# Fused attention and feed-forward kernel: one transfer for the values of the first two groups, with the order around it laid anew

## The chip, the cores and the metric

One Trainium2 chip; the program runs on one core. That core has a matrix engine (TensorE, PE in the profile), a vector engine (VectorE, DVE), an activation engine (ScalarE, ACT), a general one (GpSimd, POOL) and a sequencer that mostly starts transfers (SyncE, SP). Each of them works through its own list of instructions strictly in order. The metric is device time in microseconds (us) of one execution; lower is better.

## The reference

Attention with normalised queries and keys for 8 batches of 12 heads, 448 positions, head size 64, followed by a two-layer feed-forward block with a leaky ReLU:

```python
q_n = q / (norm(q) + 1e-06);  k_n = k / (norm(k) + 1e-06)
scores = q_n @ k_n.T / tau                      # tau = 0.1
attn = exp(scores - max);  attn = attn / (sum(attn) + 1e-09)
x = (attn @ v)                                  # heads laid side by side: 3584 x 768
h = x @ w_in                                    # 768 -> 2048
out = maximum(0.01 * h, h) @ w_out              # 2048 -> 768
```

Inputs and output are float32 in memory. Since query and key rows have length one, the kernel leaves out the subtraction of the maximum.

## The kernel before

The work is cut into many small steps, each a Python function that issues a few instructions, and one long string, `ORDER`, lists all steps of the whole run. A loop at the end of the kernel takes the names one after the other (`k.3.2` calls `scores(3, 2)`). Each engine gets its instructions in the order of the string, and the framework adds the waits that the data need. So an instruction can be held by its own data, or by one ahead of it on its engine. There is no other planning at run time.

The names that matter here. A *slot* s is a pair of heads of one batch (slots 0 to 11, the first two batches, six slots each; from slot 12 on a slot carries the queries or the keys of two pairs). A *group* j is four heads, that is slots 2j and 2j+1. A *chunk* c is 384 columns (even) or 512 columns (odd) of tokens.

- `lq.s` loads queries and keys of a slot (SP; slots 0 to 5 are loaded ahead of the string by L652 to L660, in the order of the slots). There are four buffers, so from slot 10 on the load waits until `no` of an earlier slot has read its buffer.
- `lv.j` loads the values of group j (POOL starts it; L255). The three buffers are used in turn. `lr.b.lo.hi` loads the last 64 rows of the values of batch b for heads lo to hi-1 of each group, one transfer a head (L263). `lg.g` loads values for later groups (L281).
- `wi.i` loads a quarter of w_in (POOL; L181): i = 0, 1 are the even and odd row tiles for blocks 0 to 7, i = 2, 3 for blocks 8 to 15. `wo.half.lo.hi` loads w_out (L187); `wo.0` the columns 0 to 383, `wo.1.0.8` and `wo.1.8` the two parts of the rest.
- `sq.s.part` squares (POOL; part 0 the queries, 1 the keys, L305; L299 later), `su.s.part` adds the squares up (DVE, L318, L315), `ro.s` takes logarithm and exponential of the sums (ACT, L335 and L336), `no.s` normalises (DVE, L341 to L359). `qf`, `uf` and `sa` are the same for the first slots on ACT and DVE.
- `tp.s` transposes on PE (L375), `tc.s` copies the result out of PSUM (DVE, L391; `ta` on ACT). Later slots use `tt.s` (DVE, L401) and `td.u`, six transfers on SP (L410).
- `k.s.i` computes scores (PE, L428), `x.s.i` their exponentials (ACT, L439). `to.j` adds up the exponentials of a group and `pr.j.e` multiplies them with the values (PE, L451); `ln.j`, `in.j` make the inverse of the sums (ACT, L463, L467), `sc.j.e` scales into the tile xT (DVE, L479).
- For later groups `q.u.i` (PE, L493), `y.u.i` (ACT, L501), `g.g` and `g.g.e` (PE, L525, L539), `gl.g`, `gi.g` (ACT, L547, L551), `gx.g.e` (DVE, L565, L571) do the same.
- `f.c.m` is block m of the first layer (PE, L589): six products, one for each row tile of xT; `f.c.m.0.2` does only row tiles 0 and 2. Row tile 2j+e is what `sc.j.e` wrote. `r.c.m` is the ReLU into hT (ACT, L603). `s.c.ts.lo.hi` is the second layer (PE, L625), sixteen products over all blocks of the chunk; `o` copies it out (DVE, L641) and, when the row block is complete, stores it (SP, L649).
- `w.n` issues n products on constant data (L696), which fill PE's list while data are on the way. `hs.s` lets SP's list, `hp.s` POOL's, wait until `no.s` is done (L702, L705). `tg` ends a rule on which PSUM banks are dealt out.

PSUM has eight banks. A step that needs one or two takes those that were given back longest ago in the order of the string, and its first product waits until the step that gave them back has run. `k`, `q` and `g` need two at once, `f`, `s`, `tp`, `to`, `pr` one.

Of the kernel before, what the change touches and what calls it, by code (L numbers as in the profile page):

```python
# [13 lines left out]


ORDER = """
lq.6 qf.0.0.3 qf.0.3.4 uf.0.0.3 tg sq.2.1 qf.1.0.3 uf.0.3.4 sq.2.0 w.20 lr.0.0.2 uf.1.0.3 sq.3.1 lv.0 ro.0
sa.1.0 sq.3.0 no.0 sa.1.1 tp.0.4.7 tp.0.0.4 w.2 w.2 su.1.1 su.1.0 ta.0.0.4 tc.0.4.7 su.2.1 sq.4.1 lr.0.2.4
k.0.1 k.0.2 ro.1 k.0.0 no.1 w.2 w.2 w.2 su.2.0 lv.1 x.0.2 sq.4.0 sq.5.1 wi.0 lv.2 tp.1 tc.1 k.1.0 x.0.0 x.0.1
ro.2 x.1.0 su.3.1 no.2 k.1.2 k.1.3 w.2 lq.7 sq.5.0 su.3.0 lq.9 lq.8 x.1.2 k.1.1 x.1.3 ro.3 w.2 tp.2 w.3 tc.2  # L20
su.4.1 no.3 x.1.1 k.2.2 k.2.1 to.0 tp.3 k.2.0 su.4.0 x.2.2 wi.1 x.2.1 w.2 tc.3 ln.0 ro.4 x.2.0 sq.7.1 k.3.0
su.5.1 no.4 k.3.2 k.3.1 in.0 x.3.2 x.3.1 x.3.0 su.5.0 pr.0.1 tp.4 sq.6.1 sq.6.0 k.3.3 pr.0.0 tc.4 sc.0.1 k.4.0
ro.5 x.3.3 no.5 x.4.0 to.1 ln.1 k.4.2 tp.5 k.4.1 su.6.0 su.6.1 tc.5 x.4.2 ro.6 sq.9.1 pr.1.0 k.5.1 x.4.1 in.1
no.6 sc.0.0 sc.1.0 pr.1.1 x.5.1 k.5.2 sq.7.0 tp.6 x.5.2 tc.6 k.5.0 f.0.1.0.2 wi.2 sc.1.1 k.5.3 k.6.2 x.5.0
x.5.3 su.7.1 su.7.0 su.9.1 sq.9.0 su.9.0 sq.8.0 wi.3 k.6.0 x.6.2 to.2 sq.8.1 x.6.0 ro.7 pr.2.0 pr.2.1 ln.2
k.6.1 x.6.1 su.8.1 no.7 lq.10 f.0.3.0.1.2.3 f.0.1.1 f.0.1.3 f.0.0.0.2 in.2 sc.2.0 sc.2.1 f.0.0.1 f.0.0.3
f.0.2.0.1.2.3 f.0.4 tp.7 wo.0 f.0.2.4.5 su.8.0 ro.8 f.0.3.4.5 r.0.2 f.0.6 f.0.1.4.5 f.0.0.4.5 tc.7 no.8 ro.9
r.0.6 f.0.7 lq.11 tp.8 wo.1.0.8 lr.1.0.4 sq.10.0 sq.10.1 r.0.3 r.0.1 r.0.0 r.0.4 k.7.3 k.7.2 no.9 x.7.3 x.7.2
tc.8 lv.3 sq.11.1 sq.11.0 tp.9 tc.9 su.10.1 su.10.0 ro.10 r.0.7 f.0.15 lq.13 lq.12 f.0.9 f.0.5 f.0.11 sq.12
r.0.15 r.0.9 no.10 r.0.5 k.9.0 k.7.1 k.8.2 r.0.11 f.0.12 x.9.0 r.0.12 x.8.2 tp.10 f.0.10 tc.10 su.11.0 su.11.1  # L30
x.7.1 f.0.14 hs.9 hp.10 sq.13 k.10.0 k.7.0 k.8.1 r.0.14 x.7.0 f.0.8 f.0.13 x.8.1 ro.11 r.0.10 no.11 wo.1.8
to.3 su.13 su.12 r.0.13 x.10.0 r.0.8 ln.3 ro.13 ro.12 hs.11 s.0.0.0.384 tp.11 o.0.0.0.384 k.9.1 k.10.2 k.9.3
lq.15 s.0.2.0.384 no.13 tc.11 no.12 lq.14 x.9.3 x.10.2 x.9.1 sq.15 tt.12 k.11.2 k.8.0 tt.13 x.8.0 o.0.2.0.384
k.9.2 s.0.1.0.384 lv.4 k.11.1 td.0 x.9.2 in.3 x.11.2 k.11.3 k.10.1 hp.11 sq.14 hp.12 x.11.1 x.11.3 lv.5 pr.3.0
to.4 pr.3.1 k.11.0 sc.3.0 o.0.1.0.384 su.15 lq.16 s.0.2.384.768 su.14 s.0.1.384.768 o.0.2.384.768 hp.13 sq.16
lq.17 x.10.1 x.11.0 ln.4 ro.15 in.4 q.0.1 q.0.6 no.15 sc.3.1 q.0.2 ro.14 o.0.1.384.768 pr.4.1 to.5 tt.15 y.0.6
lq.18 y.0.2 su.16 pr.5.0 ln.5 in.5 y.0.1 pr.5.1 pr.4.0 sc.4.1 sc.5.0 no.14 ro.16 sc.4.0 q.0.4 q.0.5 tt.14
sc.5.1 td.1 lq.19 s.0.0.384.768 no.16 f.1.2 hp.15 sq.18 su.18 f.1.14 f.1.1 hp.16 sq.17 lg.0 su.17 sq.19 lq.21
r.1.2 ro.18 y.0.4 y.0.5 ro.17 f.1.8 o.0.0.384.768 f.1.10 r.1.1 r.1.8 r.1.14 r.1.10 f.1.11 q.1.6 q.0.3 q.1.5
f.1.12 no.17 r.1.11 y.0.3 y.1.6 f.1.6 lq.20 tt.17 tt.16 r.1.12 y.1.5 q.0.0 q.1.4 q.1.3 y.0.0 su.19 no.18 hp.17  # L40
sq.20 ro.19 y.1.3 y.1.4 f.1.5 f.1.13 f.1.3 no.19 q.1.1 r.1.6 r.1.13 r.1.5 g.0 q.1.2 y.1.1 q.1.0 r.1.3 gl.0
tt.18 tt.19 su.20 f.1.4 f.1.0 f.1.7 sq.21 td.2 f.1.9 lq.22 td.3 lq.23 y.1.0 f.1.15 su.21 ro.21 ro.20 r.1.0
r.1.15 r.1.7 r.1.9 r.1.4 y.1.2 gi.0 g.0.0 q.2.0 s.1.0.0.384 y.2.0 gx.0.0 q.2.2 q.2.1 q.2.3 no.21 o.1.0.0.384
no.20 tt.20 s.1.1.0.384 s.1.0.384.768 tt.21 lq.24 td.4 lq.25 o.1.1.0.384 sq.23 hp.19 sq.22 y.2.2 lg.1 su.22
y.2.1 q.2.4 y.2.3 hp.20 y.2.4 q.2.5 q.2.6 y.2.5 y.2.6 s.1.1.384.768 o.1.1.384.768 ro.22 s.1.2.0.384
o.1.2.0.384 no.22 tt.22 lq.26 hp.22 sq.24 su.23 q.3.0 y.3.0 g.1 gl.1 q.3.1 q.3.2 y.3.1 o.1.0.384.768 y.3.2
gi.1 ro.23 s.1.2.384.768 o.1.2.384.768 no.23 q.3.3 y.3.3 g.1.0 gx.1.0 tt.23 td.5 lq.27 hp.23 sq.25 su.24 q.3.4
q.3.5 y.3.4 y.3.5 ro.24 s.1.3.0.384 o.1.3.0.384 q.3.6 y.3.6 g.1.1 gx.1.1 q.4.0 q.4.1 y.4.0 y.4.1 lg.2
# [52 lines left out]
def kernel(  # L101
# [145 lines left out]

    vb, vrb = {}, []

    def load_v(j):  # L250
# [4 lines left out]
        gp.dma_start(out=vb[j], in_=main(v, b, 4 * jj, 4))  # L255
# [510 lines left out]
```

## Time and profile before

| | us |
|---|---|
| median of three runs (lowest to highest) | 416.45 (416.26 to 416.78) |
| the profiled execution, its own time | 415.89 |
| its span, first to last instruction | 414.1 |
| PE busy | 404.9 |
| DVE busy | 259.4 |
| ACT busy | 245.8 |
| POOL busy | 113.2 |
| PE's last product ends (from the span's start) | 411.0 |

The profile was taken by the hardware's profiler. Times in it count from the start of the span. "Busy" is time in which an engine executes; PE's is a little generous, since its products overlap. The granted TensorE clock is full over the whole span. Bandwidth over the first 78 us is 200 to 310 GB/s nearly throughout; the transfers that POOL starts run on one queue (called q0) and those of SP on another (q1), both served by the same sixteen engines.

The chain of work that ended last, followed back from the end, is 84% PE, most of it second-layer and first-layer products:

```profile
PE 84%; DMA 9%; SPq 2%; POOL 1%; ACT 1%; DVE 1%; issue 0%; POOLq 0%
```

How long the transfers took from their start to their landing, read for single ones by line: the first values (`lv.0`, started at 12.7 us) 6.0 us, `lv.1` (16.6) 5.5, `lv.2` (20.0) 8.9; the four quarters of w_in (19.2, 21.8, 28.6, 31.4) 8.7, 11.2, 9.6 and 11.3; `wo.0` (33.0) 21.9, `wo.1.0.8` (33.8) 24.5, `wo.1.8` (55.3) 12.4; keys of slot 5 (10.4) 4.8.

### The profile page before, as it was taken

How to read it: one execution, taken by the hardware profiler on the slowest of the kernel's cores; microseconds unless marked ns; L12 is line 12 of the kernel's file. 1: busy time of each engine (PE TensorE's matmuls, PEld its weight loads, DVE VectorE, ACT ScalarE, POOL GpSimd, SP SyncE). 2: the span in 40 equal slices, each digit the busy share in tenths (PEclk: the TensorE clock that was granted, in tenths of full speed). 3: DMA queues.
4: the chain of work that ended last, by engine and by line, in shares of the span. 5: the costliest groups of instructions: out<-in, count | busy, mean ns of one | idle time of the engine just before them, and what ended most of it. 6: DMA issues, size and time to landing. Idle time of an engine off the chain costs nothing.

```text
span 414.1 us, 11068 instructions
## 1 busy us (share of the span) xinstructions
PE 404.9 (98%) x4679; PEld 212.4 (51%) x4679; DVE 259.4 (63%) x424; ACT 245.8 (59%) x431; POOL 113.2 (27%) x120
## 2 busy tenths in 40 slices
...
GB/s 188 254 217 213 242 214 219 174 220 124 71 172 174 210 111 54 184 225 106 96 135 161 170 156 167 84 206 83 2 90 79 86 40 0 2 72 6 2 115 76
DMA packets 41974, 53.81 MB, mean 130 GB/s; under 512 B 12484, under 2 KB 32324, under 8 KB 41924
## 3 DMA queue, kind: packets, MB, share of 16 engines
q1 hardware_dynamic: 25732, 41.01, 35.1%
...
q10 hardware_dynamic: 688, 0.30, 0.3%
q14 instruction: 14, 0.11, 0.1%
...
## 4 chain that ended last, share of the span: by engine, by line
PE 84%; DMA 9%; SPq 2%; POOL 1%; ACT 1%; DVE 1%; issue 0%; POOLq 0%
PE ps L625 35%; PE ps L589 32%; PE ps L539 8%; PE ps L493 7%; DMA w_out_sb<-in_moe_w_out_dram 5%; DMA qk_h<-in_k_dram 3%; PE ps L451 2%; DMA xT<-in_q_dram 1%; POOL sq L305 1%; DVE xT L571 1%; PE ps L525 1%; PE ps L428 1%; ACT hT L603 0%; SPq L210 0%; SPq L218 0%; SPq L240 0%
## 5 line engine op out<-in xcount | busy, mean ns | idle before, releaser
L625 PE MATMUL ps<-w_out_sb,hT 128*128 128x384 bf16 (+1 forms) x912 | 151.7, 324 | 0.5 <-DMA w_out_sb<-in_moe_w_out_dram 0.5
L589 PE MATMUL ps<-xT,w_in_sb 128*128 128x384 bf16 (+1 forms) x768 | 151.0, 353 | 0.2 <-DMA w_in_sb<-in_moe_w_in_dram 0.2
L501 ACT ACTIVATE pe<-ps 128x896 bf16<-128x896 f32 x126 | 109.7, 917 | 53.3 <-PE ps L493 53.1
L625 PEld LDWEIGHTS <-hT 128*128 128x128 bf16 x912 | 86.5, 98 | 64.5 <-issue 10.8
L589 PEld LDWEIGHTS <-w_in_sb 128*128 128x128 bf16 x768 | 73.3, 98 | 73.3 <-issue 7.5
L603 ACT ACTIVATE hT<-ps 128x384 bf16<-128x384 f32 (+1 forms) x128 | 63.9, 549 | 64.0 <-PE ps L589 46.0
L299 POOL TENSOR_TENSOR sq<-qk_h 128x896 f32<-128x896 f32 x36 | 64.2, 1786 | 86.8 <-DMA qk_h<-in_k_dram 51.2
L641 DVE COPY osb<-ps 128x384 f32<-128x384 f32 (+1 forms) x57 | 30.7, 543 | 76.9 <-PE ps L625 73.2
L349 DVE TENSOR_TENSOR qn<-qk_h,r 128x896 bf16<-128x896 f32 x36 | 43.8, 1216 | 1.3
L315 DVE TENSOR_REDUCE ss<-sq 128x14 f32<-128x910 f32 x36 | 38.2, 1071 | 4.6 <-POOL sq L299 4.4
L439 ACT ACTIVATE pe<-ps 128x896 bf16<-128x896 f32 x42 | 36.0, 917 | 3.3 <-PE ps L428 3.2
L493 PE MATMUL ps<-qkT 64*32 64x448 bf16 x1008 | 36.6, 353 | 0.6 <-DVE xT L571 0.6
L509 DVE TENSOR_TENSOR shared<-shared,pe 128x896 f32<-128x896 f32 x30 | 35.2, 1207 | 0.3
L565 DVE TENSOR_TENSOR xT<-ps,rb 128x448 bf16<-128x448 f32 x32 | 18.3, 615 | 20.4 <-ACT rb L551 12.4
L401 DVE STREAM_TRANSPOSE tt<-qn 128x448 f32<-128x448 f32 x36 | 28.5, 812 | 0.5
L539 PE MATMUL ps<-pe,vq 64*32 64x448 bf16 x1008 | 27.0, 349 | 0.7 <-ACT hT L603 0.7
L493 PEld LDWEIGHTS <-qkT 64*32 64x32 bf16 x1008 | 12.7, 90 | 20.0 <-issue 16.0
L341 DVE TENSOR_REDUCE r<-norms 128x14 f32<-128x28 f32 x48 | 8.4, 175 | 23.0 <-ACT norms L336 22.4
L705 POOL CAST seen<-qn 128x1 f32<-128x1 bf16 x17 | 3.1, 183 | 65.7 <-DVE qn L349 65.7
L281 POOL DMA_DIRECT2D vq<-in_v_dram x20 | 12.6, 637 | 25.6 <-PE ps L493 25.6
L539 PEld LDWEIGHTS <-vq 64*32 64x32 bf16 x1008 | 14.7, 93 | 9.6 <-issue 1.6
L335 ACT ACTIVATE ss<-ss 128x14 f32<-128x14 f32 x48 | 10.4, 216 | 13.5 <-DVE ss L315 9.9
...
## 6 DMA issues: line engine op xcount, KB each, us to landing
...
w_in_sb<-in_moe_w_in_dram POOLq DMA_DIRECT2D x4, 768.0 KB, 10.4
...
```

The lines of the kernel that those rows point to most:

```text
L299: gp.tensor_tensor(sq[:, :, :D], x, x, op=ALU.mult)
L315: nc.vector.tensor_reduce(o, sqs[s], axis=AX.X, op=ALU.add)
L349: nc.vector.tensor_tensor(qn[s].rearrange("p m d e -> p m e d"), raw[s].rearrange(f"p ({t[1:-1]} d) -> p m e d", e=n, d=D), r.rearrange(f" ...
L439: nc.scalar.activation(out=dst, in_=sc[:, :, :S], func=AF.Exp, scale=inv_tau)
L493: nc.tensor.matmul(out=sc[32 * strip : 32 * strip + 32, a, :S], lhsT=x[rows, c0 : c0 + 32], rhs=x[rows, 0:S], start=True, stop=True,)
L501: nc.scalar.activation(out=pq[u, i], in_=sc[:, :, :S], func=AF.Exp, scale=inv_tau)
L509: eng.tensor_tensor(whole[u], pq[u, 0] if i == 1 else whole[u], pq[u, i], op=ALU.add)
L539: nc.tensor.matmul(out=po[32 * strip : 32 * strip + 32, w, :S], lhsT=weights, rhs=pq[us[x if two else 0], i][rows, a, :], start=(i == 0), ...
L589: nc.tensor.matmul(out=pm[:, :n], lhsT=w_in_sb[:, kt, m * 128 : (m + 1) * 128], rhs=xT[c // 2][:, kt, c0 : c0 + n], start=(done + i == 0), ...
L603: nc.scalar.activation(out=hT[c][:, m, :n], in_=pm[:, :n], func=AF.Prelu, alpha=0.01)
L625: nc.tensor.matmul(out=po2[:, : hi - lo], lhsT=hT[c][:, m, ts * 128 : (ts + 1) * 128], rhs=w_out_sb[:, m, lo:hi], start=(m == 0), stop=(m ...
L641: nc.vector.tensor_copy(out=o[:, lo:hi], in_=bank(("s", c, ts, lo))[:, : hi - lo])
```

## The change

`load_v` gets a second argument and can load several groups in one transfer; the steps `lv.0` and `lv.1` become one step `lv.0.2`, eight heads. The string `ORDER` is laid anew from its start up to the step `q.2.4`. All other steps are the same, with the same arguments and the same number of each, and from `hp.20`, just behind `q.2.4`, the order is the same step for step; so are the other functions. In the part laid anew, all engines' lists change. Of the diff of the string, the middle of the old part is left out; the new part is complete up to `q.2.4`.

```diff
--- before
+++ after
-lq.6 qf.0.0.3 qf.0.3.4 uf.0.0.3 tg sq.2.1 qf.1.0.3 uf.0.3.4 sq.2.0 w.20 lr.0.0.2 uf.1.0.3 sq.3.1 lv.0 ro.0
-sa.1.0 sq.3.0 no.0 sa.1.1 tp.0.4.7 tp.0.0.4 w.2 w.2 su.1.1 su.1.0 ta.0.0.4 tc.0.4.7 su.2.1 sq.4.1 lr.0.2.4
-k.0.1 k.0.2 ro.1 k.0.0 no.1 w.2 w.2 w.2 su.2.0 lv.1 x.0.2 sq.4.0 sq.5.1 wi.0 lv.2 tp.1 tc.1 k.1.0 x.0.0 x.0.1
-ro.2 x.1.0 su.3.1 no.2 k.1.2 k.1.3 w.2 lq.7 sq.5.0 su.3.0 lq.9 lq.8 x.1.2 k.1.1 x.1.3 ro.3 w.2 tp.2 w.3 tc.2
-su.4.1 no.3 x.1.1 k.2.2 k.2.1 to.0 tp.3 k.2.0 su.4.0 x.2.2 wi.1 x.2.1 w.2 tc.3 ln.0 ro.4 x.2.0 sq.7.1 k.3.0
-su.5.1 no.4 k.3.2 k.3.1 in.0 x.3.2 x.3.1 x.3.0 su.5.0 pr.0.1 tp.4 sq.6.1 sq.6.0 k.3.3 pr.0.0 tc.4 sc.0.1 k.4.0
...
-r.0.6 f.0.7 lq.11 tp.8 wo.1.0.8 lr.1.0.4 sq.10.0 sq.10.1 r.0.3 r.0.1 r.0.0 r.0.4 k.7.3 k.7.2 no.9 x.7.3 x.7.2
-tc.8 lv.3 sq.11.1 sq.11.0 tp.9 tc.9 su.10.1 su.10.0 ro.10 r.0.7 f.0.15 lq.13 lq.12 f.0.9 f.0.5 f.0.11 sq.12
-r.0.15 r.0.9 no.10 r.0.5 k.9.0 k.7.1 k.8.2 r.0.11 f.0.12 x.9.0 r.0.12 x.8.2 tp.10 f.0.10 tc.10 su.11.0 su.11.1
-x.7.1 f.0.14 hs.9 hp.10 sq.13 k.10.0 k.7.0 k.8.1 r.0.14 x.7.0 f.0.8 f.0.13 x.8.1 ro.11 r.0.10 no.11 wo.1.8
-to.3 su.13 su.12 r.0.13 x.10.0 r.0.8 ln.3 ro.13 ro.12 hs.11 s.0.0.0.384 tp.11 o.0.0.0.384 k.9.1 k.10.2 k.9.3
...
-f.1.12 no.17 r.1.11 y.0.3 y.1.6 f.1.6 lq.20 tt.17 tt.16 r.1.12 y.1.5 q.0.0 q.1.4 q.1.3 y.0.0 su.19 no.18 hp.17
-sq.20 ro.19 y.1.3 y.1.4 f.1.5 f.1.13 f.1.3 no.19 q.1.1 r.1.6 r.1.13 r.1.5 g.0 q.1.2 y.1.1 q.1.0 r.1.3 gl.0
-tt.18 tt.19 su.20 f.1.4 f.1.0 f.1.7 sq.21 td.2 f.1.9 lq.22 td.3 lq.23 y.1.0 f.1.15 su.21 ro.21 ro.20 r.1.0
-r.1.15 r.1.7 r.1.9 r.1.4 y.1.2 gi.0 g.0.0 q.2.0 s.1.0.0.384 y.2.0 gx.0.0 q.2.2 q.2.1 q.2.3 no.21 o.1.0.0.384
-no.20 tt.20 s.1.1.0.384 s.1.0.384.768 tt.21 lq.24 td.4 lq.25 o.1.1.0.384 sq.23 hp.19 sq.22 y.2.2 lg.1 su.22
-y.2.1 q.2.4 y.2.3 hp.20 y.2.4 q.2.5 q.2.6 y.2.5 y.2.6 s.1.1.384.768 o.1.1.384.768 ro.22 s.1.2.0.384
+w.20 sq.2.1 qf.0.0.3 qf.0.3.4 uf.0.0.3 uf.0.3.4 qf.1.0.3 uf.1.0.3 ro.0 sa.1.0 sa.1.1 no.0 lv.0.2 tg sq.2.0
+tp.0.0.4 tp.0.4.7 ta.0.0.4 w.2 w.2 su.1.0 su.1.1 w.2 sq.3.1 sq.3.0 ro.1 tc.0.4.7 k.0.0 k.0.1 su.2.1 no.1 k.0.2
+w.3 su.2.0 x.0.1 x.0.0 tp.1 tc.1 ro.2 x.0.2 sq.4.1 lr.0.2.4 lr.0.0.2 w.2 k.1.2 k.1.1 k.1.0 no.2 sq.4.0 x.1.2
+w.2 x.1.1 su.3.0 su.3.1 sq.5.0 w.2 tp.2 k.1.3 x.1.0 ro.3 w.2 tc.2 x.1.3 su.4.1 no.3 k.2.0 k.2.1 k.2.2 x.2.0
+su.4.0 to.0 sq.5.1 su.5.0 lv.2 tp.3 tc.3 x.2.1 x.2.2 ro.4 ln.0 w.2 lq.6 lq.7 su.5.1 wi.0 k.3.2 k.3.1 sq.6.1
+wi.1 wi.2 sq.6.0 k.3.3 ro.5 pr.0.0 sq.7.0 x.3.1 x.3.2 no.4 in.0 x.3.3 no.5 pr.0.1 sq.7.1 lq.9 tp.4 k.3.0 tc.4
+x.3.0 tp.5 k.4.1 k.4.0 x.4.1 to.1 sc.0.0 tc.5 su.6.1 su.6.0 x.4.0 pr.1.1 k.4.2 sq.9.1 ln.1 ro.6 pr.1.0 x.4.2
+in.1 k.5.0 k.5.1 x.5.0 sc.0.1 su.7.1 no.6 tp.6 lq.8 sc.1.0 k.5.2 x.5.1 sc.1.1 x.5.2 f.0.1.0.2 k.5.3 tc.6 k.6.1
+k.6.2 lq.10 x.5.3 x.6.1 sq.9.0 sq.8.0 wi.3 sq.8.1 to.2 su.7.0 su.8.1 ro.7 pr.2.1 pr.2.0 wo.0 wo.1.0.8 sq.10.0
+sq.10.1 su.9.1 su.9.0 ln.2 no.7 f.0.1.1 f.0.0.0.2 f.0.3.0.1.2.3 in.2 f.0.0.3 f.0.0.1 tp.7 sc.2.0 sc.2.1 x.6.2
+f.0.6 tc.7 lq.11 su.8.0 f.0.0.4.5 k.7.3 f.0.1.3 f.0.1.4.5 f.0.7 ro.9 ro.8 r.0.0 r.0.1 x.7.3 r.0.6 f.0.4
+f.0.3.4.5 r.0.7 r.0.4 r.0.3 k.7.0 k.7.2 k.6.0 no.8 x.7.2 sq.11.1 tp.8 f.0.14 no.9 f.0.11 x.6.0 f.0.12 tp.9
+f.0.9 r.0.14 r.0.11 x.7.0 r.0.9 tc.8 tc.9 su.10.0 su.10.1 k.8.2 k.7.1 sq.11.0 f.0.5 x.7.1 r.0.12 x.8.2 f.0.10
+ro.10 r.0.10 lq.12 lq.13 hs.9 wo.1.8 f.0.15 k.9.2 sq.12 lv.3 k.8.1 r.0.15 k.8.0 x.9.2 su.11.1 x.8.1 x.8.0
+su.11.0 f.0.13 f.0.8 no.10 f.0.2.0.1.2.3 ro.11 r.0.8 f.0.2.4.5 to.3 r.0.13 k.9.1 lr.1.0.4 sq.13 r.0.5 k.9.0
+ln.3 no.11 r.0.2 lq.14 tp.10 tp.11 s.0.2.0.384 su.12 ro.12 x.9.0 x.9.1 tc.11 tc.10 k.11.1 in.3 k.9.3 k.10.2
+o.0.2.0.384 no.12 su.13 s.0.1.0.384 x.11.1 x.10.2 ro.13 sq.14 tt.12 hp.12 lv.5 hp.10 lv.4 k.11.2 k.10.0 x.9.3
+s.0.0.0.384 x.11.2 x.10.0 s.0.0.384.768 hs.11 lq.15 sq.15 o.0.1.0.384 o.0.0.0.384 no.13 su.15 o.0.0.384.768
+k.11.3 k.11.0 k.10.1 hp.11 lq.17 su.14 tt.13 to.4 pr.3.1 lq.18 x.11.3 x.11.0 x.10.1 pr.3.0 to.5 pr.4.1 ro.14
+ln.5 ro.15 sc.3.0 sc.3.1 pr.5.0 pr.5.1 pr.4.0 no.14 no.15 td.0 in.5 ln.4 s.0.1.384.768 tt.15 tt.14 hp.15 sq.18
+s.0.2.384.768 lq.16 in.4 sc.5.0 td.1 o.0.1.384.768 q.0.2 sc.5.1 sc.4.0 sc.4.1 sq.17 sq.16 hp.13 q.0.1 q.0.0
+su.17 o.0.2.384.768 su.18 y.0.1 lq.21 f.1.7 f.1.13 y.0.0 ro.17 y.0.2 r.1.13 r.1.7 no.17 su.16 f.1.1 f.1.15
+lq.19 hp.17 sq.21 r.1.1 q.1.3 q.1.6 ro.18 r.1.15 q.1.4 f.1.11 f.1.4 y.1.3 y.1.4 y.1.6 r.1.4 ro.16 r.1.11 f.1.6
+r.1.6 sq.19 lg.0 q.0.3 q.0.4 su.21 no.16 q.1.1 y.1.1 y.0.4 f.1.3 f.1.5 y.0.3 f.1.14 r.1.5 su.19 no.18 f.1.2
+tt.17 tt.16 ro.21 r.1.14 r.1.2 f.1.12 no.21 lq.20 ro.19 r.1.3 sq.20 q.0.6 hp.16 y.0.6 r.1.12 q.0.5 q.1.2
+f.1.10 f.1.8 f.1.9 td.2 y.0.5 y.1.2 f.1.0 r.1.8 lq.22 r.1.9 q.1.5 r.1.10 y.1.5 su.20 r.1.0 no.19 g.0 q.2.0
+q.1.0 g.0.0 gl.0 gi.0 ro.20 y.1.0 y.2.0 s.1.0.0.384 lq.23 q.2.1 gx.0.0 q.2.2 q.2.3 tt.19 tt.18 o.1.0.0.384
+tt.21 no.20 s.1.0.384.768 s.1.1.0.384 tt.20 lq.24 td.3 td.4 lq.25 sq.23 hp.19 y.2.2 sq.22 y.2.3 lg.1 su.22
+q.2.4 o.1.1.0.384 y.2.1 hp.20 y.2.4 q.2.5 q.2.6 y.2.5 y.2.6 s.1.1.384.768 o.1.1.384.768 ro.22 s.1.2.0.384
...
     vb, vrb = {}, []

-    def load_v(j):
-        if j >= B * NQ:
-            return
+    def load_v(j, n=1):
         b, jj = divmod(j, NQ)
-        vb[j] = v_old[:, j % 3]
-        gp.dma_start(out=vb[j], in_=main(v, b, 4 * jj, 4))
+        for i in range(n):
+            vb[j + i] = v_old[:, (j + i) % 3]
+        gp.dma_start(
+            out=v_old[:, j % 3 : j % 3 + n].rearrange("p j h t d -> p (j h) t d"),
+            in_=main(v, b, 4 * jj, 4 * n),
+        )

     def load_v_rem(b, heads=range(4)):
         if b >= B:

```

The order of POOL's list up to the last part of w_out, written out. Before: sq.2.1 sq.2.0 lr.0.0.2 sq.3.1 lv.0 sq.3.0 sq.4.1 lr.0.2.4 lv.1 sq.4.0 sq.5.1 wi.0 lv.2 sq.5.0 wi.1 sq.7.1 sq.6.1 sq.6.0 sq.9.1 sq.7.0 wi.2 sq.9.0 sq.8.0 wi.3 sq.8.1 wo.0 wo.1.0.8 lr.1.0.4 sq.10.0 sq.10.1 lv.3 sq.11.1 sq.11.0 sq.12 hp.10 sq.13 wo.1.8. After: sq.2.1 lv.0.2 sq.2.0 sq.3.1 sq.3.0 sq.4.1 lr.0.2.4 lr.0.0.2 sq.4.0 sq.5.0 sq.5.1 lv.2 wi.0 sq.6.1 wi.1 wi.2 sq.6.0 sq.7.0 sq.7.1 sq.9.1 sq.9.0 sq.8.0 wi.3 sq.8.1 wo.0 wo.1.0.8 sq.10.0 sq.10.1 sq.11.1 sq.11.0 wo.1.8 sq.12 lv.3 lr.1.0.4.

More of the change, by code (lines that the diff above doesn't have):

```diff
@@ L22 @@
-su.5.1 no.4 k.3.2 k.3.1 in.0 x.3.2 x.3.1 x.3.0 su.5.0 pr.0.1 tp.4 sq.6.1 sq.6.0 k.3.3 pr.0.0 tc.4 sc.0.1 k.4.0
[L23 to L26, printed above, removed]
```

8 lines of the change are left out of this document (removed).

## Prediction

> **What bounds the kernel now.** I read the engine shares first, then what TensorE (PE) waited for, then its busy time by stretches, then the timeline at each wait. First line: busy time and share of the span. Below it, who PE waited for (total, times, longest, in us).
>
> ```profile
> PE 404.9 (98%) x4679; PEld 212.4 (51%) x4679; DVE 259.4 (63%) x424; ACT 245.8 (59%) x431; POOL 113.2 (27%) x120
> ```
> ```profile
> PE ps L375 <- DVE qn L359: 1.4, 3, 0.7
> PE ps L428 <- DVE qkT L391: 0.7, 1, 0.7
> PE ps L539 <- ACT hT L603: 0.7, 1, 0.7
> PE ps L493 <- DVE xT L571: 0.6, 1, 0.6
> PE ps L625 <- DMA w_out_sb<-in_moe_w_out_dram: 0.5, 1, 0.5
> PE ps L589 <- DMA w_in_sb<-in_moe_w_in_dram: 0.2, 1, 0.2
> ```
>
> PE idles 414.1 - 404.9 = 9.2 us: 1.7 before its first product, 3.1 after its last, 4.5 between. The stretches (start:end, length, then busy PE, PEld, DVE, ACT, POOL) say where:
>
> ```profile
> 10.00:20.00 10.00, 8.69 (x75) 3.67 (x74) 9.58 (x23) 9.23 (x19) 9.95 (x14) 1.00 1.16 252
> 20.00:30.00 10.00, 9.52 (x126) 4.27 (x125) 9.63 (x22) 9.94 (x18) 8.37 (x10) 1.00 1.19 219
> 30.00:40.00 10.00, 9.98 (x109) 5.57 (x108) 9.13 (x20) 7.23 (x17) 7.50 (x10) 1.00 1.09 212
> ...
> 100.00:110.00 10.00, 9.31 (x103) 4.61 (x102) 1.98 (x3) 6.04 (x13) 0.79 (x1) 1.00 0.39 93
> 110.00:120.00 10.00, 9.39 (x96) 4.93 (x94) 8.54 (x15) 4.64 (x7) 4.04 (x6) 1.00 0.57 112
> ```
>
> From 10 to 33 us VectorE (DVE), ScalarE (ACT) and GpSimd (POOL) are full and PE follows them. From 33.9 PE has first-layer products enough and waits only for weights (0.2 at 42, 0.5 at 54.9) and at 106 to 112 (0.69 + 0.61). Both orders hold the same products and fillers (w.20, eight w.2, one w.3), and are the same from q.2.4 on, which before starts at 117.7. Only waits ahead of it can change: at best -4.5 us, with no such bound upward.
>
> **The change, part by part.** I follow the new order with the durations of the old timeline.
>
> *One value transfer.* Two issues of 0.81 and 0.78 become one of 1,024 rows, which the trace doesn't have: at least one (0.8), at most both (1.6). The w_out issues of as many or twice the rows took 0.88 to 1.22, so 1.0: POOL saves 0.6, which the next part uses up.
>
> *POOL, 9 to 21 us.* Before:
>
> ```profile
> 10.53 1.42 POOL L263 DMA_DIRECT2D shared<-in_v_dram  x2
> 11.96 0.84 POOL L305 TENSOR_TENSOR sq<-xT 128x384 f32<-128x384 f32 x1
> 12.74 0.81 POOL L255 DMA_DIRECT2D shared<-in_v_dram  x1
> 13.57 1.83 POOL L305 TENSOR_TENSOR sq<-xT 128x512 f32<-128x512 f32 x2
> 15.34 1.29 POOL L263 DMA_DIRECT2D shared<-in_v_dram  x2
> ```
>
> The value transfer now goes at 9.6, ahead of sq.2.0, which ends at 11.6; DVE wants it at 11.96, so 0.4 is left. All four lr (1.42 + 1.29 = 2.7) now stand between sq.4.1 and sq.4.0. POOL reaches sq.4.1 at 13.4, but slot 4's k, issued at 9.42, lands like the next one (4.8 later) at about 14.2. So: sq.4.1 14.4 to 15.2, lr to 17.9, sq.4.0 to 19.0, sq.5.0 to 20.0, sq.5.1 to 20.9. DVE took su.4.0 at 18.64: it waits 0.4, and since su.5.0 now stands ahead of tc.3, tc.3 slips from 19.36 to 20.8; su.5.1 ends at 21.9.
>
> Price of the early transfer for the loads: when value packets came in, the SP queue's packets fell. Packets, MB, share, at 10 to 12 and then at 12 to 14 us:
>
> ```profile
> q1 hardware_dynamic: 845, 0.47, 94.1%
> ```
> ```profile
> q1 hardware_dynamic: 593, 0.43, 77.4%
> q0 software_dynamic: 150, 0.02, 14.3%
> ```
>
> 0.04 to 0.07 MB lost per 2 us, over the 4 us that 1,024 packets take at the 454 to 513 per 2 us of later stretches: about 0.1 MB, 0.5 us at 0.24 MB/us. The bounds are 0 and 2 (all of the values' 0.39 MB ahead of slot 4's k); I take 0.3 into the sum. The Trainium skill (DMA: Bandwidth & Descriptors, Queues, rings and completion order) has each DMA engine take turns between queues packet by packet. The trace agrees (845 to 593 beside 150); taken strictly, one turn for each of 1,024 packets, it gives the 2 us end, +1.4 on the sum, as rival 2.
>
> *ACT, 12 to 33 us.* It is full (9.94 of 10), so a wait here delays all behind it. ro.2 now stands ahead of x.0.2 and waits for su.2.0 (12.4 to 12.7: 0.3); ro.5 ahead of x.3.1 waits for su.5.1 (20.8 to 21.9: 1.1), with all exponentials of slot 3 queued behind. Before it idled 0.2 here. So x.5.3, which ended at 31.5 (28.32 + 4 x 0.80), ends at 32.9; to.2 and pr.2, 0.95 + 1.5 on PE, follow, and the run of first-layer products starts at 35.1 for 33.9. Between the bounds 34.4 (ro.5 doesn't wait) and 36.8 (2 us later loads) I take 35.1.
>
> *PE, 35 to 43 us.* To its first upper block (f.0.14) the new order holds 34 matmuls of 0.163 (the chain of waits has 0.97 us for six; 5.5 in all), four score steps of 0.25 and two transposes of 0.45: 7.4. It arrives at 42.5. That block needs the last w_in quarter, which (time from issue to landing, by line) left at 31.36 and landed 11.3 later, at 42.7; before, PE came to it thus:
>
> ```profile
> 42.72 3.53 PEld L589 LDWEIGHTS <-w_in_sb 128*128 128x128 bf16 x23 [0.47 <-DMA w_in_sb<-in_moe_w_in_dram]
> ```
>
> The weight queue runs without a gap from 22 us (0.30 to 0.43 MB per 2 us). By 22 it had moved 0.51 MB before; the new order issues wi.0 later (21.7 for 19.2) but has the first values behind it then, and wi.2 at 25 for 28.6 only deepens a queue that never empties. So 42.7 again (41.7 to 43.7), and the gate swallows most of ACT's loss. But by that gate the old order had done f.0.2 (0.98) and tp.9 (0.45) more, and k.7.0 (0.23) less: **+1.2**, and +0.3 for loads and gate.
>
> *w_out.* From f.0.14 to the first second-layer product: ten f of 0.98, to.3 0.95, seven scores 1.6, three transposes 1.35 = 13.7, so 43.0 + 13.7 = 56.7. wo.0 landed at 54.8; lq.14 goes out ahead of hold hs.11 (about 52 for 57.1), 0.23 MB, 1 us at 0.2 MB/us: 55.8. The wait of 0.5 goes: **-0.5** (+0.5 if wo.0 comes at 57.7).
>
> *57 to 105 us.* No wait before, none found now; tightest: pr.3.1 (PE at 70.0) takes the bank of copy o.0.0.384.768, on DVE behind no.13 and su.15 (ends 69.6): 0.4 left. td.0, now behind the first output store, lq.17 and lq.18 on SP, lands at 78 for 80.6; wo.1.8 goes out at 49 for 55.3 and lands at about 64 for 67; lr.1 and lv.3, now behind it, at about 66 for 70. hp.13, behind sq.16, frees no.17 at 83.4 with nothing late. **0** (to +1.5).
>
> *105 to 112 us.* Before:
>
> ```profile
> 106.42 1.52 PE L539 MATMUL ps<-pe,vq 64*32 64x448 bf16 x56 [0.69 <-ACT hT L603]
> ...
> 112.12 0.38 PE L493 MATMUL ps<-qkT 64*32 64x448 bf16 x7 [0.61 <-DVE xT L571]
> ```
>
> g.0.0 took the bank that r.1.15 gives, late on ACT; q.2.3 takes the banks of gx.0.0, whose inverse gi.0 stood behind r.1.4 and y.1.2. Now gi.0 follows gl.0, and g.0.0 plus a whole s (2.6) lie between: gx.0.0 (2.55) ends as q.2.2 starts. **-1.3** (0 if gi.0 is late again).
>
> Sum: 1.2 + 0.3 - 0.5 - 1.3 = **-0.3 us**. Span 413.8; the profiled execution took 415.89, so 415.6; the three runs' median, 416.45, lies 0.56 above it: **416.1**.
>
> **Rivals.**
> 1. *Faster: weights come earlier and ACT loses less.* I could place the landing of wi.3 only to 1 us. If wi.3 lands at 41.7 and the product run starts at 34.4, f.0.14 starts at 41.8: -1.2 more, 414.9. For it: wi.2 out 3.5 us earlier, fewer value issues among the weights. Against: the queue had no gap to fill.
> 2. *Slower: the value transfer holds up slot 4.* If k of slot 4 lands 2 us late, sq.4.1 to sq.5.1, tc.3, ro.5 and the exponentials slip, the products start at 36.8, f.0.14 at 44.2: 1.2 over my 43.0, and it counts from 43 on, since nothing refills. With 0.2 more waits of PE on tc.3, +1.1: 417.5. For it: SP packets fell by 30% beside few value packets. Against: fewer bytes than in 14 to 20 us, where landings stayed at 4.3 to 4.8.
> 3. *Slower: a new bank wait at 70 us.* If sq.15 comes 1.5 late, su.15 holds the copy and pr.3.1: +1.3, 417.4. Against: lq.15 goes out at the same 56.
> 4. *The transfer isn't the matter*: with the waits at 106 kept, 417.4; counted within 3.
>
> The Trainium skill (SBUF - State Buffer, SBUF: two separate sides) warns that VectorE instructions in a two-port mode keep GpSimd from writing descriptors. No row bears it out: an L255 issue took 0.78 at 16.6 with DVE 93% busy and 0.82 at 43.4 with DVE 61% busy; a hold would act as rival 2 and is counted there.
>
> **From these to the numbers.** Forecast 0.36 (415.3 to 417.2), rival 1 0.30, rival 2 0.20, rivals 3 and 4 together 0.14. A measurement here tells about 0.2% (0.8 us) from nothing. Faster: rival 1 and the low edge of the forecast, 0.32; slower: rivals 2 to 4 and its upper edge, 0.36; same 0.32. The range goes from rival 1 with 0.5 to spare, 414.4, to rivals 2 and 3 together, 418.8.
>
> **What would show it.** The value issue at 9.6 near 1.0 us; su.4.0 waiting for POOL; an ACT wait of about 1 at ro.5; first-layer products from 35; f.0.14 waiting for w_in near 42.7; no wait at the first second-layer product (56.7); none at 105 to 112; q.2.4 at 117.4. I am wrong if f.0.14 starts before 42 or after 44, or if PE shows a wait over 0.5 between 57 and 117.

## The result, and the profile after

| | before | after |
|---|---|---|
| median, us (four runs each, one chip) | 416.36 (415.87 to 416.78) | 424.09 (423.19 to 424.78) |
| ratio, 95% interval | | 1.0176 (1.0154 to 1.0199) |
| profiled execution, us; its span | 415.89; 414.1 | 424.04; 422.3 |
| TensorE idle in the span, us | 9.2 | 16.6 |
| first-layer run of products starts | 33.91 | 34.83 |
| first second-layer product | 54.86 | 65.22 |
| q.2.4, from which both orders agree | 117.73 | 125.26 |

The changed kernel is 1.8% slower, 5 us above the top of the predicted range. The shares of the profile's page, and then the waits of TensorE from 30 us on (engine and line, whom it waited for, total us, times, longest):

```profile
PE 405.7 (96%) x4662; PEld 213.2 (50%) x4679; DVE 258.0 (61%) x424; ACT 246.5 (58%) x431; POOL 112.9 (27%) x119
```
```profile
PE ps L377 <- DVE qn L361: 7.3, 2, 6.9
PE ps L591 <- DVE xT L567: 0.5, 1, 0.5
PE ps L591 <- issue: 0.5, 3, 0.2
PE ps L627 <- DVE osb L643: 0.2, 1, 0.2
```

Nearly all of the loss is one wait of 6.9 us. The waits of before at 54.9, 106 and 112 us are gone, as forecast. The stretches (columns as in the prediction; the last three are TensorE's granted clock, the busy share of the DMA engines and GB/s) place the loss:

```profile
30.00:40.00 10.00, 6.31 (x80) 3.08 (x79) 2.19 (x4) 5.83 (x10) 2.65 (x4) 1.00 0.96 199
40.00:50.00 10.00, 6.68 (x35) 3.65 (x36) 6.82 (x15) 3.20 (x9) 3.85 (x4) 0.66 1.15 183
100.00:110.00 10.00, 9.89 (x87) 4.48 (x89) 8.11 (x13) 8.45 (x17) 4.63 (x5) 1.00 0.44 94
110.00:120.00 10.00, 10.00 (x193) 5.04 (x191) 5.60 (x9) 7.60 (x13) 2.69 (x5) 1.00 0.65 162
```

GpSimd stands from 28.7 to 37.3 us, VectorE from 32.2 to 40.0, ScalarE from 35.9 and TensorE from 36.5 on. From 36.5 to 37.3 no engine works, so they wait for something from outside. The chain that ended last, from 24 to 44 us (start, us, what), says for what:

```profile
24.01 13.20 DMA qk_h<-in_k_dram
...
37.33 1.04 POOL sq L307
38.37 0.74 POOL w_in_sb L181
...
39.14 0.85 POOL sq L307
...
40.01 1.63 DVE ss L320 x3
...
42.72 0.56 DVE qn L361
43.28 0.04 issue
43.32 0.91 PE ps L377 x7
```

Read backwards: the transposes of slot 7 (tp.7, L377) wait for no.7 on VectorE, which stands behind the sums of slots 8 and 9 (three reductions at 40.01); the first of these is su.8.1, which needs sq.8.1, and that stands on GpSimd behind sq.8.0 and wi.3. GpSimd stood 8.6 us at sq.8.0, waiting for the last of slot 8's loads, the remainder of k that went out at 24.01: `load_qk` puts the remainders of q and of k (L240) into the tile that sq.8.0 squares. The rows that sq.8.1 itself reads had landed at 34.1 (22.40 + 11.7). So the order on GpSimd has a share in the stall: with sq.8.1 ahead of sq.8.0 it could have run at 34.1 instead of 39.1, an estimate from this trace that no run tests. Slot 7 and slot 9 had long been ready. wi.3 and w_out behind sq.8.0 went out 7 us later than before.

Why was slot 8 late? SP's queue in the changed kernel, with slot 8's four loads last (from 21.26 on):

```profile
15.43 0.61 SPq L240 DMA_DIRECT2D qk_h<-in_q_dram  x1
16.81 0.59 SPq L240 DMA_DIRECT2D qk_h<-in_k_dram  x1
18.07 0.38 SPq L237 DMA_DIRECT2D qk_h<-in_q_dram  x1
19.35 0.37 SPq L238 DMA_DIRECT2D qk_h<-in_k_dram  x1
19.85 0.61 SPq L240 DMA_DIRECT2D qk_h<-in_q_dram  x1
20.50 0.61 SPq L240 DMA_DIRECT2D qk_h<-in_k_dram  x1
21.26 1.10 SPq L237 DMA_DIRECT2D qk_h<-in_q_dram  x1
22.40 0.47 SPq L238 DMA_DIRECT2D qk_h<-in_k_dram  x1
22.91 1.05 SPq L240 DMA_DIRECT2D qk_h<-in_q_dram  x1
24.01 0.92 SPq L240 DMA_DIRECT2D qk_h<-in_k_dram  x1
```

Slot 8's four loads before:

```profile
18.36 0.59 SPq L237 DMA_DIRECT2D qk_h<-in_q_dram  x1
19.04 0.43 SPq L238 DMA_DIRECT2D qk_h<-in_k_dram  x1
19.51 0.61 SPq L240 DMA_DIRECT2D qk_h<-in_q_dram  x1
20.16 0.60 SPq L240 DMA_DIRECT2D qk_h<-in_k_dram  x1
```

The last two, whose landings the profile of before has, took 6.9 and 7.5 us and were there by 27.7. After, the issue at 18.07 falls on the landing of the eighth before it (issued 10.95, 7.1 us on the way), the one at 19.35 on that of 11.47 + 7.9, the one at 19.85 on that of 11.98 + 7.9. The trace says why: SP's loads use eight semaphores (signals that count landings) in turn, and each issue first waits for the semaphore of the eighth before it. The one at 18.07, for instance, waits for semaphore 103, which the load of 10.95 raised. So the program itself lets eight of SP's transfers be on the way at a time, and slower landings hold up what comes later. Before, the loads issued from 10.96 to 12.63 took 4.3 to 4.9. Of the 2.9 us by which slot 8's first load is late, 0.8 come from two issues that took longer (1.00 and 1.05 us at 11.98 and 13.02, 0.61 and 0.60 before); most of the rest are these waits.

The issues at 22.40 and 22.91 then took 11.7 and 12.7 us to land, while those of 19.35 to 20.50, only 2 to 3 us earlier, took 4.2 to 4.7. Between the two groups the weights had gone out: wi.0 at 20.64, wi.1 at 22.18, and wi.2 followed at 22.98.

### The profile page after: what moved, and what is told of

Same layout as the page of the kernel before. It is cut to its first block, busy times and chain, and to the rows that moved or that the text cites. A ratio compares the mean times of both kernels' runs of the same rounds, so it can differ in the third digit from the quotient of the medians.

```text
span 422.3 us, 11053 instructions
## 1 busy us (share of the span) xinstructions
PE 405.7 (96%) x4662; PEld 213.2 (50%) x4679; DVE 258.0 (61%) x424; ACT 246.5 (58%) x431; POOL 112.9 (27%) x119
## 4 chain that ended last, share of the span: by engine, by line
PE 84%; DMA 7%; SPq 3%; DVE 3%; issue 1%; ACT 1%; POOL 1%; DVEq 0%; POOLq 0%
PE ps L591 34%; PE ps L627 33%; PE ps L541 7%; PE ps L495 6%; DMA qk_h<-in_k_dram 3%; DMA qk_h<-in_q_dram 2%; PE ps L453 2%; PE ps L430 1%; DMA xT<-in_q_dram 1%; DMA qkT<-tt 1%; SPq L240 1%; PE ps L377 1%; DVE tt L403 1%; PE ps L527 1%; SPq L210 0%
## 5 line engine op out<-in xcount | busy, mean ns | idle before, releaser
L301 POOL TENSOR_TENSOR sq<-qk_h 128x896 f32<-128x896 f32 x36 | 63.1, 1758 | 78.6 <-DMA qk_h<-in_k_dram 42.9
L351 DVE TENSOR_TENSOR qn<-qk_h,r 128x896 bf16<-128x896 f32 x36 | 44.8, 1245 | 1.4
L441 ACT ACTIVATE pe<-ps 128x896 bf16<-128x896 f32 x42 | 35.9, 916 | 4.7 <-PE ps L430 4.7
L511 DVE TENSOR_TENSOR shared<-shared,pe 128x896 f32<-128x896 f32 x30 | 34.1, 1169 | 0.3
L567 DVE TENSOR_TENSOR xT<-ps,rb 128x448 bf16<-128x448 f32 x32 | 18.3, 617 | 20.5 <-ACT rb L553 12.4
L707 POOL CAST seen<-qn 128x1 f32<-128x1 bf16 x17 | 4.1, 239 | 73.7 <-DVE qn L351 73.7
L495 PEld LDWEIGHTS <-qkT 64*32 64x32 bf16 x1008 | 12.8, 90 | 18.5 <-issue 14.4
L283 POOL DMA_DIRECT2D vq<-in_v_dram x20 | 12.7, 639 | 24.7 <-PE ps L495 24.7
```

What stands on the lines that cost most here:

```text
L301: gp.tensor_tensor(sq[:, :, :D], x, x, op=ALU.mult)
L351: nc.vector.tensor_tensor(qn[s].rearrange("p m d e -> p m e d"), raw[s].rearrange(f"p ({t[1:-1]} d) -> p m e d", e=n, d=D), r.rearrange(f" ...
L441: nc.scalar.activation(out=dst, in_=sc[:, :, :S], func=AF.Exp, scale=inv_tau)
L495: nc.tensor.matmul(out=sc[32 * strip : 32 * strip + 32, a, :S], lhsT=x[rows, c0 : c0 + 32], rhs=x[rows, 0:S], start=True, stop=True,)
L511: eng.tensor_tensor(whole[u], pq[u, 0] if i == 1 else whole[u], pq[u, i], op=ALU.add)
```

## The experiments

Three theories: the early value transfer is what makes slot 8 late (A); the three w_in quarters that the new order has on the way by 23.8 us (before two) starve slot 8's loads (B); the order on VectorE and GpSimd turns a late load into a stall (C). All runs were made beside runs of before on the same chip. One table, to be read with the texts below: "values" is the issue of the first value transfers, "6/7" the landing time of slot 6's k load (L238, issued near 11.3), then the issue of slot 8's q remainder (L240) and the time that it took to land, TensorE's longest wait after 30 us, and the median of all runs (range).

| run | values | 6/7 | slot 8's q remainder out, us to land | wait, for | us |
|---|---|---|---|---|---|
| before | 12.74 | 4.9 | 19.51, 6.9 | 0.7 | 416.36 |
| after | 9.84, eight heads | 7.9 | 22.91, 12.7 | 6.9, tp.7 | 424.09 (423.19 to 424.78) |
| e1_split | 9.56, four and four | 8.5 | 23.37, 13.3 | 7.8, tp.7 | 425.06 (424.53 to 425.87) |
| e2_old_places | 11.31, 16.55 | 5.4 | 19.68, 4.8 | 0.5, w_in | 415.29 (414.41 to 415.57) |
| e3_wi2_late | 9.35, eight | 7.0 | 21.61, 11.8 | 5.4, tp.7 | 422.28 (420.32 to 424.96) |
| e5_su8_late | 9.50, eight | 8.0 | 22.77, 13.8 | 3.5, ScalarE | 420.51 (420.14 to 422.21) |
| e4_old_early | 9.71, eight | 7.5 | 22.67, 9.8 | 2.2, xT | 421.33 (418.67 to 422.13) |
| e6_single_mid | 11.88, eight | 4.5 | 20.53, 4.5 | 0.2 | 416.38 (414.05 to 420.45) |
| e7_single_late | 16.14, eight | 4.1 | 19.37, 5.4 | 0.4 | 418.94 (415.62 to 420.80) |
| e8_half_early | 9.88, 16.91 | 8.2 | 23.18, 12.9 | 6.7, tp.7 | 416.15 (415.07 to 423.11) |
| e10_weights_behind | 9.61, eight | 8.6 | 23.28, 4.1 | 3.6, w_in | 419.18 (418.49 to 420.78) |
| e9_best | 11.20, 16.62 | 5.9 | 20.18, 9.0 | 1.0, w_in | 414.93 (414.70 to 415.69) |
| e11_wi3_early | 11.94, 17.18 | 4.6 | 19.62, 4.4 | 0.7, tp | 415.26 (414.37 to 415.51) |

**The form of the transfer (e1_split).**

```diff
- ... no.0 lv.0.2 tg ...
+ ... no.0 lv.0 lv.1 tg ...
```


> The new order, with the values of the two groups in two transfers of four heads, one behind the other, at the place of the single one. If the place and the bytes of the early values are what holds up the queue of SP: slot 8's loads again go out behind 21 us and land behind 34, the transposes of slot 7 again wait 4 to 8 us near 36, 422 to 426 us. If the form of the single transfer of eight heads is what counts (10.7 us to land, against 5.5 to 6.0 for four heads before): each half lands in 6 to 7 us, slot 8's loads land before 31, and the time is 415 to 418 us.

424 to 426 came: the form isn't the matter, the place and the bytes are. Two issues cost GpSimd 1.70 us for 1.08 and all is a little later than after.

**Values at their old places (e2_old_places).** Everything else of the new order stays.

```diff
- ... no.0 lv.0.2 tg ...
- ... w.2 sq.3.1 sq.3.0 ...
- ... lr.0.2.4 lr.0.0.2 w.2 ...
+ ... no.0 tg ...
+ ... w.2 sq.3.1 lv.0 sq.3.0 ...
+ ... lr.0.2.4 lr.0.0.2 lv.1 w.2 ...
```


> The new order, with the two value transfers at their old places (behind the squares of slot 3, near 13 us, and behind the first loads of the remainder, near 17 us). If the early values hold up the queue of SP: loads of slots 6 and 7 land in 4 to 6 us, slot 8's last load goes out before 22 us and lands before 32, the wait at the transposes of slot 7 is under 2.5 us, and the time is 416 to 419 us. If the three quarters of w_in that are on the way by 23 us starve slot 8's loads by themselves: these still take 10 us or more and land behind 33, the wait is over 3.5 us, and the time is 420 to 424 us.

Theory A, and better than it said: 415.29, below before (ratio 0.9965, 0.9949 to 0.9980), 8.8 us below after. TensorE's timeline (start, us, idle before in brackets):

```profile
34.32 1.64 PE L591 MATMUL ps<-xT,w_in_sb 128*128 128x384 bf16 x9
35.80 0.55 PE L377 MATMUL ps<-id,qn 128*128 128x128 bf16 x7
...
42.66 2.94 PE L591 MATMUL ps<-xT,w_in_sb 128*128 128x384 bf16 x17 [0.47 <-DMA w_in_sb<-in_moe_w_in_dram]
...
56.31 2.76 PE L627 MATMUL ps<-w_out_sb,hT 128*128 128x384 bf16 x16
```

The transposes of slot 7 come at 35.80, not at 43.32, with wi.2 as early as in the changed kernel. So B by itself does no harm: slot 8's loads went out ahead of the quarters here (the q remainder at 19.68, wi.0 at 20.91). Against after the 8.8 us at q.2.4 (116.49 for 125.26) are: 0.5 at the start of the run, 7.0 more up to the transposes, and 1.4 from there to the second layer (20.5 for 21.9 us), which is the clock, below.

**The old order with early values (e4_old_early).** The new `load_v` comes with it.

```diff
- ... sq.2.1 qf.1.0.3 ... sq.3.1 lv.0 ro.0 ... su.2.0 lv.1 x.0.2 ...
+ ... sq.2.1 lv.0.2 qf.1.0.3 ... sq.3.1 ro.0 ... su.2.0 x.0.2 ...
```


> The order of before throughout, with one edit: the values of the two groups come in one transfer of eight heads behind the k squares of slot 2 (near 9.5 us), as in the changed kernel, and no longer near 12.7 and 16.6 us. If the early values alone hold up SP's queue and the late slot 8 then holds up VectorE, whatever the rest of the order: slot 8 lands behind 32 us, TensorE waits 3 to 6 us near 37 us at the transposes of slot 7, and the time is 419 to 423 us. If it takes the new order as well (three quarters of w_in early): slot 8 lands before 31 us, and the time is 415 to 418 us.

The first of the two: 421.33 (ratio 1.0092, 1.0058 to 1.0125). Slot 8's last load goes out at 23.32 for 20.16 and takes 10.9 us for 7.5; VectorE waits 3.31 us at su.8.1, and TensorE 2.2 us, at a first-layer product near 40 us whose input VectorE makes behind no.7. That is less than the 3 to 6 expected; the profiled execution, 418.94, is one of the two shortest of the five. The early values do this in either order.

**How many bytes, and when (e6_single_mid, e7_single_late, e8_half_early).** The new order with the single transfer behind sq.3.1, with it behind lr.0.0.2, and with lv.0 early and lv.1 behind lr.0.0.2.

```diff
- ... no.0 lv.0.2 tg ...
+ ... sq.3.1 lv.0.2 sq.3.0 ...
```
```diff
- ... no.0 lv.0.2 tg ...
+ ... lr.0.0.2 lv.0.2 w.2 ...
```
```diff
- ... no.0 lv.0.2 tg ...
+ ... no.0 lv.0 tg ... lr.0.0.2 lv.1 w.2 ...
```


> The new order, with the single transfer of eight heads some 1.5 us later, behind the k squares of slot 3 (near 11.3 us), where the first of the two transfers stood before. If what counts is that value bytes are on the way ahead of the loads of slots 4 to 7, in proportion to their number: between the two kernels, slot 8 lands at 31 to 35 us, 417 to 422 us. If only a transfer at 9.8 us does harm: slot 8 lands before 31, 415 to 416.5 us.

> The new order, with the single transfer of eight heads behind the first loads of the remainder (near 16.5 us), where the second transfer stood before. If the early bytes are the cause: loads of slots 6 and 7 land in 4 to 5.5 us, slot 8's before 31.5. The first value products then wait for the values, which land at 24 to 26 us, by 2 to 4 us at 21.5; of this 0 to 1.5 us reaches the first layer's run (34.3 us with the values at their old places), and the time is 414.5 to 417.5 us. If the form of eight heads is the cause: slot 8 lands behind 33 us and the time is 420 us or more.

> The new order, with half of the values early: the first group's four heads at the place of the single transfer (near 9.5 us), the second group's behind the first loads of the remainder (near 16.5 us). If the harm goes by the bytes that are early: slot 8 lands at 31 to 34 us, the wait at the transposes of slot 7 is 1 to 4 us, 417 to 421 us. If half of them are covered (a threshold: SP's eight transfers in flight are not filled up by them): slot 8 lands before 31, no wait there, 414.5 to 416 us.

None of the three did as expected; their executions jump. e6, the same 384 KB only 2 us later, ran from 414.05 to 420.45 (ratio, without this longest one, 0.9990, 0.9962 to 1.0018). e8 ran seven times at 415.07 to 417.36 and once at 423.11. This last one is the execution with the profile, and is left out of the ratio (0.9986, 0.9971 to 1.0001): it shows the whole stall of the changed kernel, and the other seven, 6 to 8 us shorter, can hardly have had it. I take it that each execution decides anew whether slot 8 falls on the good or the bad side, and that the amount and time of the early values move the odds. This is not shown, since each kernel has the profile of one execution only. e7 keeps SP's queue free, as expected; the first value products wait 1.2 us and the first-layer run starts at 36.55, for 34.32 in e2. That is its price in the profiled execution, of 416.25. The median, 418.94, is 2.7 us higher and above the 414.5 to 417.5 expected, and what the longer executions lose beyond that price stays open.

**The weights ahead of slot 8's loads (e3_wi2_late, e10_weights_behind).** wi.2 behind sq.9.0; then all of wi.0 to wi.2 behind sq.7.1.

```diff
- ... wi.1 wi.2 sq.6.0 ... sq.9.0 sq.8.0 ...
+ ... wi.1 sq.6.0 ... sq.9.0 wi.2 sq.8.0 ...
```
```diff
- ... su.5.1 wi.0 k.3.2 k.3.1 sq.6.1
- wi.1 wi.2 sq.6.0 ... sq.7.1 lq.9 ...
+ ... su.5.1 k.3.2 k.3.1 sq.6.1
+ sq.6.0 ... sq.7.1 wi.0 wi.1 wi.2 lq.9 ...
```


> The new order, with the third quarter of w_in behind the k squares of slot 9 (near 28.7 us, where before had it), so that two quarters and not three are on the way when slot 8's loads go out. If the quarters starve these loads: they still go out at 21 to 24 us, but land in 7 to 9 us, before 33; the wait at the transposes of slot 7 falls from 6.9 to under 3 us, and the time is 417 to 420 us. If the values alone are the cause: slot 8 still lands behind 35, the wait stays over 5 us, 422 to 425 us.

> The new order with the early single transfer, and the first three quarters of w_in behind the k squares of slot 7 on GpSimd (near 24.5 us instead of 20.6 and 22.2), so behind slot 8's loads. If these loads are late in two steps, 3 us by SP's queue and the rest by the weights ahead of them: they still go out at 21 to 24 us but land in 4.5 to 7 us, by 30 us and not at 36.7; TensorE doesn't wait for slot 7's transposes; instead it waits 1.5 to 5 us near 30.5 to 34 for the first quarter, and the time is 416 to 420 us. If the early values hold these loads up by themselves: they take 10 us and more, land behind 33, and the time is 422 us or more.

In e3 slot 8's loads of 21.08 and 21.61, behind the first quarter (20.27) and just ahead of the second (21.80), still take 10.9 and 11.8 us, and the wait is 5.4, for 6.9 with the third quarter early. This profile is of the shortest of four executions (420.32 to 424.96), so the 1.5 us are not shown to be the third quarter's. In e10, with none ahead, the loads go out as late as ever (21.63 to 24.13), but the two with a landing in the profile take 4.9 and 4.1 and are there by 27.4. The time from issue to landing of one load, slot 8's q remainder (L240), issued at 22.91 in the changed kernel:

```profile
DMA to landing us min/median/max: 12.7/12.7/12.7
```

and issued at 23.28 in e10_weights_behind:

```profile
DMA to landing us min/median/max: 4.1/4.1/4.1
```

As expected, the lateness has two steps: 3 to 4 us on SP's queue beside the values, and then 8 us more because the load falls among weights on the way. TensorE waits in e10 for the weights instead, 3.6 us at the first first-layer products:

```profile
34.48 0.82 PE L591 MATMUL ps<-xT,w_in_sb 128*128 128x384 bf16 x2 [3.62 <-DMA w_in_sb<-in_moe_w_in_dram]
```

**The order on VectorE (e5_su8_late).**

```diff
- ... su.7.0 su.8.1 ro.7 ... tc.7 lq.11 su.8.0 ...
+ ... su.7.0 ro.7 ... tc.7 su.8.1 su.8.0 lq.11 ...
```


> The new order, with only the sums of slot 8 moved: both behind the copy of slot 7's transposes on VectorE instead of ahead of slot 9's sums and slot 7's normalising. The loads are as in the changed kernel. If the late load costs time because the sums of slot 8 stand ahead of ready work on VectorE: slot 7's transposes start at 35.5 to 37 us instead of 43.3, the granted clock of 40 to 48 us is over 0.9, and what is left is a wait of up to 2.5 us near 43 us, at the transposes of slot 8 or at the first product with the fourth quarter of w_in (46 us); 415 to 419 us. If the late load itself is what counts, and order on VectorE not: a wait of 5 us or more turns up elsewhere before 47 us, and the time stays at 421 to 425 us.

Half of it, between the two times expected. The transposes of slot 7 start at 35.78, as theory C says, though slot 8 is as late as ever. But 5 us later the same load stops the next engine, in ScalarE's and in TensorE's timeline:

```profile
42.19 0.21 ACT L337 ACTIVATE ss<-ss 128x14 f32<-128x14 f32 x1 [6.98 <-DVE ss L320]
```
```profile
44.27 0.59 PE L430 MATMUL ps<-qkT 64*64 64x448 bf16 x4 [3.45 <-ACT pe L441]
```

ro.8, which needs slot 8's sums, heads ScalarE's queue, and x.7.3, which frees a bank of scores, stands behind it. 3.6 us of 7.7 came back (420.51).

**A version for use (e9_best, e11_wi3_early).** e2 with wi.3 ahead of sq.8.0, and with wi.3 behind wi.2.

```diff
- ... sq.9.0 sq.8.0 wi.3 sq.8.1 ...
+ ... sq.9.0 wi.3 sq.8.0 sq.8.1 ...
```
```diff
- wi.1 wi.2 sq.6.0 ... sq.8.0 wi.3 sq.8.1 ...
+ wi.1 wi.2 wi.3 sq.6.0 ... sq.8.0 sq.8.1 ...
```


> The new order, with the two value transfers at their old places, and the fourth quarter of w_in ahead of the q squares of slot 8 on GpSimd (issued near 28.6 us instead of 29.6). The wait of 0.5 us for that quarter near 42 us goes; the squares of slot 8 start 0.8 us later, which nothing waits for. If so: 414.2 to 415.4 us, ratio to before 0.994 to 0.998, no wait of TensorE over 0.3 us from 34 us to the end. If the quarter's landing hangs on what else is on the way and not on its issue: the wait stays at 0.4 to 0.6, 414.8 to 415.8 us.

> The new order, with the two value transfers at their old places, and the fourth quarter of w_in directly behind the third on GpSimd (near 24 us instead of 29.6). With the quarter 1 us earlier it landed no earlier (43.2 against 42.7 us). If the quarters stand in one line on the DMA engines: it lands behind the third quarter (37.4 us) by some 4 us, at 40 to 42, so that the wait of 0.5 to 1.0 us near 42 us is gone; slot 8's loads, most of which go out before 22 us, land before 31; 414 to 415 us, ratio to before 0.992 to 0.997. If one more quarter on the way holds up slot 8's last loads: they land behind 32 us, a wait of 2 us or more stands at slot 7's transposes, 417 us or more.

Times as expected, 414.93 (0.9954, 0.9936 to 0.9971) and 415.26 (0.9959, 0.9944 to 0.9974), not to be told from e2, but not by way of the wait that the edits were to remove. The fourth quarter lands at 42.7 in before, 42.6 in e2, 43.2 in e9 and 42.5 in e11, though issued at 31.4, 29.6, 28.6 and 24.6. In e9 the wait for it is 1.0 and not gone; in e11 it is gone only because the run had started 0.7 later. All three beat both kernels by about 0.4% and 2%.

## Why the prediction was wrong

The step that failed is "Price of the early transfer for the loads": 0.04 to 0.07 MB lost per 2 us, 0.5 us of delay with bounds 0 and 2, looked for at slot 4's k only, 0.3 in the sum. Measured against e2, which takes the early transfer out, it cost 8.8 us. Three things in it were wrong.

- *Size.* Packets, MB and share of SP's queue (q1) and of GpSimd's (q0) from 12 to 14 us, in the changed kernel and then in e2:

```profile
q1 hardware_dynamic: 353, 0.25, 50.2%
q0 software_dynamic: 207, 0.08, 36.8%
```
```profile
q1 hardware_dynamic: 750, 0.54, 95.8%
q0 software_dynamic: 1, 0.00, 0.2%
```

SP moved 0.29 MB less in these 2 us than in e2 and 0.18 less than before, where I had read 0.04 from a stretch of before in which q0 carried 150 packets with 0.02 MB. The four loads issued from 10.95 to 13.02 were on the way for 7.1 to 7.9 us, the same four for 4.3 to 4.9 before and 4.2 to 5.4 in e2. The Trainium skill (DMA: Bandwidth & Descriptors, Queues, rings and completion order) has the engines take turns by packets. Taken strictly that had given the 2 us end, nearer than the value I chose. The trace of the changed kernel agrees roughly, 492 packets of q0 beside 337 of q1 in the next 2 us, 14 to 16:

```profile
q0 software_dynamic: 492, 0.19, 77.0%
q1 hardware_dynamic: 337, 0.25, 49.8%
```

Together these are 829 packets, for 751 in e2 at 12 to 14, but 0.44 MB for 0.54, since a value packet carries 0.39 KB and one of SP's 0.74. From 12 to 14 only 560 packets went through, 0.33 MB, and what held back the others stays open. Two readings of mine were loose. That SP fell from 845 packets to 593 beside 150 is no exchange of one for one. And the stretches of before from 14 to 22 hold 367 to 513 value packets, not 454 to 513, so that 1,024 take 4 to 5.6 us.
- *Place.* Slot 4's k was on time (issued 9.41, 3.4 us on the way). The delay fell on slots 6 and 7, on which nothing hung, and through the eight semaphores it reached slot 8, last in the queue. I followed the transfer to the next consumer, not to the end of its queue.
- *What it fell upon.* I wrote that wi.2 at 25 us "only deepens a queue that never empties", and weighed that for wi.3 alone, not for the loads that share the engines. A load 3 to 4 us late met the weights and became 9 us late (slot 8's q remainder, there at 35.6 for 26.4); I had given su.8.1, ahead of no.7 in both orders, no wait, since before it had none.

The rest can be read in e2, where this step is taken out:

- POOL's walk: forecast issue 1.0 us, 1.08 in the changed kernel. Right. VectorE was to wait 0.4 us for POOL at su.4.0. In the changed kernel it doesn't (18.93): slot 4's k had landed at 12.8, not at 14.2, and POOL reached the four lr at 14.5, not at 15.2. e2 has this wait, 0.40 at 18.43, but there lv.1 stands ahead of sq.4.0 too.
- ScalarE: a wait of 1.1 us at ro.5 forecast; 0.90 in e2, none in the changed kernel. Run of products at 35.1, not before 34.4; 34.83 after, 34.32 in e2, just outside. So the changed kernel met this time without the waits that were to cause it, which is luck.
- f.0.14 at 43.0 behind wi.3 at 42.7: 42.66, with a wait of 0.47. Right.
- First second-layer product at 56.7 without a wait: 56.31. Right.
- No wait from 57 to 105, none at 105 to 112, q.2.4 at 117.4: longest 0.2 us, q.2.4 at 116.49. Right, 0.9 early. The span forecast, 413.8, stands against 412.7.
- Rival 2 named the mechanism, that the values hold up loads, and missed its place (slot 8, not 4) and its size (8.8 us on e2, not 1.4). My reason against it, that landings of before stayed at 4.3 to 4.8 beside more bytes at 14 to 20 us, held for that stretch and not for this one. Why 384 KB at 9.8 us do what 192 KB at a time don't is not settled. In e2 the values slow SP just as much, to 0.24 MB from 14 to 16 us, but for one such stretch instead of two in a row. e6 has two again, 0.22 and 0.23 MB from 14 to 18, and its profiled execution loses nothing by them, so the moment counts too.
